# Attention, token mixing and routed experts on one core: separate query buffers for the last rows, earlier queries for the first full pair, a third buffer for a key load

## The chip, the core and the metric

The kernel runs on one NeuronCore of a Trainium2 chip. The metric is the device time of one execution in microseconds (us), here the median of three runs. The engines are named as the profile names them: PE (TensorE; PEld is its weight load), DVE (VectorE), ACT (ScalarE), POOL (GpSimd) and SP (SyncE), which here only issues DMAs. Each engine takes its instructions in the order in which the program gives them to it and waits on semaphores of the others.

## The reference

Attention with a position bias, then two feed-forward blocks. The change lies in the attention; the rest is cut to its signature.

```python
def _attn_ref(q, k, v, w1, b1, w2):          # q, k, v: batch 2, 8 heads, 576 rows, 64 wide
    B, H, S, D = q.shape
    scores = (1.0 / np.sqrt(D)) * np.matmul(q, k.transpose(0, 1, 3, 2))
    pos = np.arange(S)
    psi_rel = np.log1p(np.abs((pos[:, None] - pos[None, :]).astype(np.float32)))
    psi_i = np.log1p(np.maximum(pos[:, None].astype(np.float32), 1.0))
    h = np.maximum((psi_rel / psi_i)[..., None] @ w1 + b1, 0.0)   # 32 hidden values per pair of positions
    scores = scores + (h @ w2).transpose(2, 0, 1)[None]           # one bias per head
    attn = np.exp(scores - np.max(scores, axis=-1, keepdims=True))
    attn = attn / (np.sum(attn, axis=-1, keepdims=True) + 1e-09)
    return np.matmul(attn, v).astype(np.float32)

def reference(**kwargs):
    x = attention output, laid out as batch, row, head * 64
    x = _moe_ref(x, ...)       # mixes tokens, then channels
    return _moe2_ref(x, ...)   # one of 8 experts per token
```

## The kernel before

The attention runs first and is written out as 40 steps, `steps` in `attention`. A step is one block of query rows (`it`) and one `i` from 0 to 7, which names a batch and a pair of heads. The first eight steps (0 to 7) take the block `it = 4`, the last 64 rows of each head: 576 is four blocks of 128 rows and a rest of 64. For them a query tile holds two heads of 64 rows each, both for `hi` and `lo` parts, with zeros in the places of the other head. Steps 8 to 15 take `it = 0`, the first full block of 128 rows, and so on to step 39.

Each step does, for its pair of heads: the score matmuls (`scores`, L359), the bias added and the maximum taken on DVE (L337), the exponential on ACT (L340), the normalisation (L370, L371, and L374 on POOL for the last rows), the transposition of the probabilities (L387, L397, L410), the product with the values (L425) and the transposition of the result (L441). The pieces belong to different steps at a time: step s does the scores of step s, the transpositions of step s - 1 and the values of step s - 2.

Beside that, steps 0 to 7 prepare what comes later:

- **Keys.** `load_k(i)` loads the keys of two pairs by five DMAs (L216 four times, L217) into a ring of two buffers named `kn`; `key_T` transposes them on PE, casts to K on ACT (L193), and `key_split` takes the rests on DVE (L272). There are four loads: 0 and 2 at the start, 4 later in the start, 6 after step 1.
- **Queries.** `load_q` loads them into a ring of two buffers `qn`. For the last rows, one load brings four steps' worth, and `tail_split` (on POOL, L193 and L295) and `tail_T` prepare one step at a time, two steps and one step ahead. For full rows one load brings two steps; `query_T` transposes them on PE (L314) and scales them on ACT into `qr` (L197), `query_split` casts them (L193, on ACT or POOL in turn), and `query_rest` takes the rest on POOL (L325) and issues four DMAs (L328) that lay hi and lo parts out in the query tile `qt0` or `qt1`. The tiles serve the last rows and the full rows alike, so the four DMAs of the first full pair wait for scores of the last rows that read the same tile. `query_zero` (L287, L288) zeroes their empty places once, on POOL.
- **Bias.** The bias of a block of rows is made in eight groups of 16 rows. `bias_hidden` makes the hidden values (L487, L490), `bias_mm` multiplies them (L500), ACT evicts the result into one of two buffers `ev` (L503), and one DMA (L511) lays it out in the block's bias tile. The buffer `ev` of a group may be written again when the DMA of the group two before has landed. One group of block 0 is made in the start, the other seven in steps 0 to 6. Softmax of step 8 needs all eight.

All DMAs named here are issued by SP, in the order in which the code calls them; those on one queue stand behind each other. The order inside a step is a list of names, `ORDER`: "first" for steps 0 to 2, "mixed" for 3 to 7, then "bias" and "edge". The DMA of `load_q` stands ahead of the list, `load_k(6)` and `load_v(1)` behind it. Later stages (token mixing, channel mixing, routing and experts) are not touched by the change.

These are the lines that set when the queries of full rows are prepared and loaded:

```python
QO = 3, 3, 3, 6
two = lambda d: (s + d) % 2 == 0 and s + d >= B * NP and at(d)     # B * NP is 8
"query_T": (query_T, two(QO[0])), "query_split": (query_split, two(QO[1])), "query_rest": (query_rest, two(QO[2])),
if two(QO[3]):
    load_q(*steps[s + QO[3]])
```

So the first full pair (steps 8 and 9) is loaded in step 2 and prepared in step 5; the second pair (10 and 11) is loaded in step 4, into the `qn` buffer that still holds the queries of steps 4 to 7, and prepared in step 7.

Of the kernel before, what the change touches and what calls it, by code (L numbers as in the profile page):

```python
# [9 lines left out]
F32 = mybir.dt.float32  # L10
F32R = mybir.dt.float32r
# [10 lines left out]
B, H, S, D = 2, 8, 576, 64  # L22
# [29 lines left out]
AHEAD = 1  # L52
QRB = 2
TB = 2
QO = 3, 3, 3, 6

ORDER = {
    "start": "hidden0 const load_k2 tail_split0 hidden1 bias0 hidden2 bias1 key_T00 hidden3 zero key_T01 key_T11 key_T10 key_split0 tail_split1 bias2 hidden4 bias3 load_k4 hidden5 key_split1 tail_T bias4 load_v load_q".split(),
    "first": "scores0 hidden2 last_T prob_T0 values key_T0 normalize query_T tail_T query_split hidden1 hidden0 key_T1 bias_mm key_split out_T tail_split hidden3 query_rest".split(),
    "mixed": "hidden2 scores0 values tail_T query_T normalize hidden0 last_T prob_T0 key_T0 key_T1 query_split tail_split hidden1 key_split query_rest bias_mm out_T hidden3".split(),  # L60
    "bias": "query_T query_split hidden3 scores0 scores1 last_T values hidden0 query_rest hidden2 late bias_mm out_T mix prob_T0 prob_T1 hidden1 normalize".split(),
# [71 lines left out]
def attention(tc, nc, tok, mix, q, k, v, w1, b1, w2, c_L, c_id, ident, x, wt1, wt2, prefill):  # L133
# [4 lines left out]
    NP = H // 2  # L138
# [4 lines left out]
    tw_p = pool(tok, "tokw")  # L143
    with ExitStack() as ctx:
        cst = pool(ctx, "acst")
        bias_p = pool(ctx, "bias", 2)
        nat_p = pool(ctx, "nat")
# [5 lines left out]
        def alloc_ps():  # L153
            return ps_t.tile([128, 512], F32, name="tp", tag="tr")
# [40 lines left out]
        def scaled(what, out, in_):  # L195
            if next(turns[what]) == "A":
                nc.scalar.activation(out, in_, AF.Copy, scale=0.125)  # L197
            else:
                nc.vector.tensor_scalar(out, in_, 0.125, None, ALU.mult)  # L199
# [10 lines left out]
        def load_k(i):  # L210

            b, pr = divmod(i, NP)
            n = nat_p.tile([128, 20, D], F32, name="kn", tag="kn", bufs=2)
            main, hs = n[:, 0:16].rearrange("p (n h) d -> p n h d", h=4), k[b, 2 * pr:2 * pr + 4]
            for j in range(NIT):
                nc.sync.dma_start(main[:, j], hs[:, 128 * j:128 * j + 128].rearrange("h p d -> p h d"))  # L216
            nc.sync.dma_start(n[0:64, 16:20], hs[:, 512:S].rearrange("h p d -> p h d"))  # L217
            for j in range(2):
                nat["k", i + j] = main[:, :, 2 * j:2 * j + 2], n[0:64, 16 + 2 * j:18 + 2 * j]
# [14 lines left out]
        def load_q(it, i):  # L234

            b, pr = divmod(i, NP)
            n = nat_p.tile([128, 4, D], F32, name="qn", tag="qn", bufs=2)
            if it == NIT:
                tv = q[b, :, 512:S].rearrange("(a e) p d -> e p a d", e=2)
                for e in range(2):  # L240
                    nc.sync.dma_start(n[64 * e:64 * e + 64], tv[e])
                for j in range(NP):
                    nat["q", it, i + j] = n[:, j]
            else:
                nc.sync.dma_start(n, q[b, 2 * pr:2 * pr + 4, 128 * it:128 * it + 128].rearrange("h p d -> p h d"))
                nat["q", it, i] = n
# [29 lines left out]
        QT = {}  # L276
        qts = [nat_p.tile([128, 2, 4, 128], F32R, name=f"qt{i}") for i in range(2)]

        def query_tile(s):
            return qts[s // 2 % 2][:, s % 2]  # L280

# [1 line left out]

        def query_zero():

            for qt in qts:
                nc.gpsimd.memset(qt[:, :, 0:2, 64:128].bitcast(F32), 0.0)  # L287
                nc.gpsimd.memset(qt[:, :, 2:4, 0:64].bitcast(F32), 0.0)  # L288

        def tail_split(it, i):  # L290
            n = nat.pop(("q", it, i))
# [5 lines left out]

        def tail_T(it, i):
            qs = nat.pop(("qs", it, i)).bitcast(F32).rearrange("p a d -> p (a d)")
            QT[it, i] = qt = query_tile(i)  # L300
            tp = alloc_ps()
            for a in range(2):
                nc.tensor.transpose(tp[:, 128 * a:128 * a + 128], qs[:, D * a:D * a + 128], ident)
            tv = tp[:, 0:256].rearrange("p (a i) -> p a i", a=2)
            scaled("qT0", qt[:, 0:2, 0:64], tv[:, :, 0:64])
            scaled("qT1", qt[:, 2:4, 64:128], tv[:, :, 64:128])
# [277 lines left out]
        steps = [(it, i) for it in its for i in range(B * NP)]  # L584
# [23 lines left out]
        def late_fetch(s):  # L608

            if pieces and any(f is decode for f, *_ in late.get(s, ())):  # L610
                fetch(pieces.pop(0))

        load_const()
        bias_setup()
        start = {
            "const": (bias_const,), "zero": (query_zero,), "load_k2": (load_k, 2), "load_k4": (load_k, 4), "load_v": (load_v, 0),
            "load_q": (load_q, *steps[NP]), "tail_T": (tail_T, *steps[0]),
        }
        for n in range(2):
# [11 lines left out]
        for s in range(N + 2):  # L631

            bias = gi < len(groups) and s < N and s >= B * NP * (its.index(groups[gi] // 8) - 1)
            at = lambda d, n=N: steps[s + d] if 0 <= s + d < n else None
            two = lambda d: (s + d) % 2 == 0 and s + d >= B * NP and at(d)
            hide = groups[gi + 1] if bias and gi + 1 < len(groups) else None
            todo = {
                "late": (late_step, (s,)), "mix": (mixes[s][0], mixes[s][1:]) if s in mixes else (None, None),
                "tail_split": (tail_split, at(2, B * NP)), "tail_T": (tail_T, at(1, B * NP)),
                "query_T": (query_T, two(QO[0])), "query_split": (query_split, two(QO[1])), "query_rest": (query_rest, two(QO[2])),  # L640
                "key_split": (key_split, at(2, B * NP)),
                "normalize": (normalize, at(0)), "last_T": (last_T, at(-1)),
                "values": (values, at(-2)), "out_T": (out_T, at(-2)),
                "bias_mm": (bias_mm, (groups[gi],) if bias else None),
            }
            for j in range(4):
                todo[f"hidden{j}"] = bias_hidden, hide is not None and (hide, (j,))
                todo[f"key_T{j}"] = key_T, j < 2 and at(2, B * NP) and (*at(2), j)
                todo[f"scores{j}"] = scores, at(0) and (*at(0), j)
                todo[f"prob_T{j}"] = prob_T, at(-1) and (*at(-1), j)  # L650
            if two(QO[3]):
                load_q(*steps[s + QO[3]])
            for name in ORDER["edge" if bias and s % (B * NP) == B * NP - 1 else "first" if s < 3 else "mixed" if s < B * NP else "bias" if bias else "plain"]:
                f, a = todo[name]
                if a:
                    f(*(a[1:] if f in (key_split, key_T) else a))
            gi += bias
            late_fetch(s - 1)
            if s == 1:
                load_k(6)  # L660
            if s == 2:
                load_v(1)
            if s == 10:
                prefill()
            if s == 8:
                for _ in range(2):
                    fetch(pieces.pop(0))
# [1095 lines left out]
```

## Time and profile before

| | |
|---|---|
| median of 3 runs | 584.0 us (583.43 to 585.43) |
| the profiled execution, its own time | 584.03 us |
| its span, first to last instruction | 582.3 us |
| mean granted TensorE clock | 0.979 |
| busy: PE, PEld, DVE, ACT, POOL | 545.5 (94%), 430.3 (74%), 383.9 (66%), 329.5 (57%), 242.1 (42%) us |
| chain that ended last, by engine | PE 65%; DVE 12%; DMA 7%; issue 5%; ACT 5% |

The span is what lies between the first and the last instruction of the profiled execution; the rest of its 584.03 us lies around it. PE is busy 94% of the span, but not evenly: in 40 slices of the span, the first five show 7, 6, 8, 9 and 6 tenths and nearly all others 9. The steps 0 to 8 lie there: the scores of step 0 run at 21.6 us, those of step 8 at 64.5 and 66.2 us.

### The profile page before, as it was taken

The page shows a single profiled execution, that of the slowest core. Times are in us where ns is not written, and L with a number is a line of the kernel's source. Part 1 is how long each engine was busy: PE and PEld are TensorE (multiplying, and loading weights), DVE is VectorE, ACT ScalarE, POOL GpSimd, SP SyncE. Part 2 cuts the span into 40 slices and gives each one's busy share as a digit, 9 for nine tenths or more (in the row PEclk, how much of TensorE's full clock was granted, in tenths as well). Part 3 has the DMA queues.
Part 4 walks back from the last instruction along what each step waited for, and adds up shares of the span by engine and source line. Part 5 has one row for each costly group of instructions (what it writes and reads, how often), then busy time and mean ns, then how long its engine had stood idle before and what let it go on. Part 6 is the DMA issues. An engine that isn't in the chain of part 4 may idle for free.

```text
span 582.3 us, 11959 instructions
## 1 busy us (share of the span) xinstructions
PE 545.5 (94%) x4306; PEld 430.3 (74%) x4306; DVE 383.9 (66%) x896; ACT 329.5 (57%) x608; POOL 242.1 (42%) x230
## 2 busy tenths in 40 slices
PE   7689699999899999989999999999999999999992
PEld 3366477777677887869999877787778778787871
DVE  5789588889887675698888535714473235668650
ACT  4678589789898793344444223221423257777760
POOL 4666547476555360044444300310014234657541
PEclk8979889999999999999999999999999999999997
DMA  6997988698697351143443020081002985566950
GB/s 162 130 173 126 142 158 165 132 177 157 127 147 126 77 154 38 37 138 120 148 161 126 1 91 0 1 302 61 19 18 43 370 299 175 147 230 245 367 185 12
DMA packets 72110, 79.90 MB, mean 137 GB/s; under 512 B 36822, under 2 KB 51420, under 8 KB 72044
## 3 DMA queue, kind: packets, MB, share of 16 engines
q1 hardware_dynamic: 67276, 73.72, 50.7%
q0 software_dynamic: 2176, 5.26, 2.7%
q8 instruction: 36, 0.59, 0.5%
q10 hardware_dynamic: 2592, 0.09, 0.3%
q14 instruction: 30, 0.25, 0.2%
HBM read 72.08 MB, written 5.34 MB: 133 GB/s over the span
## 4 chain that ended last, share of the span: by engine, by line
PE 65%; DVE 12%; DMA 7%; issue 5%; ACT 5%; SPq 2%; POOL 2%; ACTq 0%; POOLq 0%; DVEq 0%
PE ph L748 20%; PE po L748 16%; DMA bias<-ev 6%; PE py L748 5%; PE ps L500 5%; PE tp L425 4%; PE ps L359 3%; PE tp L410 3%; DVE t L337 2%; ACT t L340 2%; PE tp L748 1%; DVE K L272 1%; DMA mt<-meta 1%; PE tp L1448 1%; DVE raw L732 1%
## 5 line engine op out<-in xcount | busy, mean ns | idle before, releaser
L490 POOL TENSOR_SCALAR hd<-tabs,sc,negb 128x576 f32<-128x576 f32 x32 | 76.4, 2389 | 4.7 <-PE ps L500 3.0
L340 ACT ACTIVATE t<-t,st 128x576 f32<-128x576 f32 x72 | 55.4, 770 | 28.8 <-DVE st L337 28.4
L748 PE MATMUL po<-cw,h 128*128 128x512 f32 x272 | 67.3, 395 | 0.0
L337 DVE CUSTOM_DVE_ANT_0 t<-ps,bias 128x576 f32<-128x576 f32 x72 | 52.3, 751 | 16.1 <-DMA bias<-ev 6.6
L359 PE MATMUL ps<-K,qt 128*128 128x288 f32 x320 | 54.0, 309 | 4.4 <-DVE qt L199 3.5
L748 PEld LDWEIGHTS po<-cw,h 128*128 128x128 f32 x272 | 49.8, 188 | 10.0 <-issue 0.4
L1411 DVE TENSOR_TENSOR big<-raw,big 128x1024 fp32r<-128x1024 f32 x30 | 42.3, 1433 | 22.4 <-ACT big L1410 22.4
L500 PE MATMUL ps<-hd,wblk 128*32 128x288 f32 x576 | 47.7, 440 | 7.5 <-DVE st L337 6.5
L359 PEld LDWEIGHTS ps<-K,qt 128*128 128x128 f32 x320 | 45.0, 192 | 6.7 <-DVE qt L199 2.3
L425 PE MATMUL tp<-pt,v 128*64 128x128 f32 (+1 forms) x800 | 49.2, 268 | 0.6 <-DVE K L272 0.6
L748 PE MATMUL py<-big,hT 128*128 128x512 f32 x184 | 47.8, 400 | 0.4 <-POOL big L1411 0.4
L1189 POOL DMA_INDIRECT meta<-tokid,posi x10 | 10.0, 996 | 90.7 <-DVE tokid L1186 54.7
L425 PEld LDWEIGHTS tp<-pt,v 128*64 128x64 f32 x800 | 40.1, 137 | 8.1 <-issue 5.1
L1410 ACT CAST big<-raw 128x1024 fp32r<-128x1024 f32 x44 | 44.2, 1055 | 2.8 <-DMA big<-in_moe_w_dram 1.0
L748 PE MATMUL ph<-big,xT 128*128 128x512 f32 x168 | 42.9, 403 | 0.0
L490 DVE TENSOR_SCALAR hd<-tabs,sc,negb 128x576 f32<-128x576 f32 x69 | 42.2, 640 | 1.0 <-PE ps L500 0.9
L748 PEld LDWEIGHTS py<-big,hT 128*128 128x128 f32 x184 | 33.8, 188 | 8.6 <-POOL big L1411 0.9
L740 POOL TENSOR_TENSOR big<-wf,big 128x512 fp32r<-128x512 f32 x12 | 18.8, 1564 | 50.3 <-ACT big L739 50.3
L487 ACT ACTIVATE hd<-tabs,b1c,sc 128x576 f32<-128x576 f32 x43 | 36.9, 866 | 3.8 <-DVE sc L458 3.7
L1411 POOL TENSOR_TENSOR big<-raw,big 128x1024 fp32r<-128x1024 f32 x10 | 27.5, 2747 | 24.9 <-ACT big L1410 24.3
L748 PEld LDWEIGHTS ph<-big,xT 128*128 128x128 f32 x168 | 30.6, 189 | 8.6 <-issue 1.6
L500 PEld LDWEIGHTS ps<-hd,wblk 128*32 128x32 f32 x576 | 17.2, 115 | 24.1 <-DVE st L337 7.9
(302 smaller groups left out, 1204.7 us busy)
## 6 DMA issues: line engine op xcount, KB each, us to landing
raw<-in_moe_w_dram SPq DMA_DIRECT2D x48, 512.0 KB
raw<-in_moe_w_ch_dram SPq DMA_DIRECT2D x24, 512.0 KB
bias<-ev SPq DMA_DIRECT2D x32, 288.0 KB
qt<-qs SPq DMA_DIRECT2D x64, 128.0 KB
lw<-in_moe_w_dram SPq DMA_DIRECT2D x16, 512.0 KB
big<-in_moe_w_dram SPq DMA_DIRECT2D x8, 512.0 KB
lw<-in_moe_w_dram SPq DMA_DIRECT2D x16, 256.0 KB
big<-in_moe_w_dram SPq DMA_DIRECT2D x16, 256.0 KB
```

The costliest lines, as they stand in the source:

```text
L337: nc.vector.tensor_tensor_reduce(t.rearrange("p (a j) -> p a j", a=2), ps[:, :, 0:HALF], bs.rearrange("p (a j) -> p a j", a=2), op0=ALU.ad ...
L340: nc.scalar.activation(t, t, AF.Exp, bias=st[:, j:j + 1], scale=-1.0, accum_out=st[:, 2 + j:3 + j])
L359: nc.tensor.matmul(ps[:, hf, 0:HALF], lhsT=qt[:, j], rhs=K[k][:, hf * HALF:(hf + 1) * HALF], start=j == pairs[0][0], stop=j == pairs[-1][0])
L410: nc.tensor.transpose(tp[:, 128 * j:128 * j + 128], tt[:, o:o + 128], ident)
L425: nc.tensor.matmul(po[64 * h:64 * h + 64, 0:rhs.shape[1]], lhsT=lhsT, rhs=rhs, start=j == 0, stop=j == 4)
L487: nc.scalar.activation(hd[:, qq], Lt[:, o:o + S], AF.Relu, bias=b1c, scale=sc[:, c])
L490: eng.tensor_scalar(hd[:, qq], Lt[:, o:o + S], sc[:, c], negb, ALU.mult, ALU.max)
L500: nc.tensor.matmul(ps[32 * qq:32 * qq + 32, hf, 0:HALF], lhsT=wblk, rhs=hd[:, qq, hf * HALF:(hf + 1) * HALF], start=True, stop=True)
L740: nc.gpsimd.tensor_tensor(lo, src, hi.bitcast(F32), ALU.subtract)
L748: nc.tensor.matmul(out, lhsT=lhs[a], rhs=rhs[b], start=first and i == 0, stop=last and i == 2)
L1410: nc.scalar.copy(hi, raw)
L1411: (nc.gpsimd if c == 3 and t else nc.vector).tensor_tensor(lo, raw, hi.bitcast(F32), ALU.subtract)
```

## The change

Three things:

- The last rows' queries get a tile of their own with two halves, `lastq`, in the place where a later weight tile (`w2s`) is allocated; `tail_T` writes it and `query_zero` zeroes it. `qt0` and `qt1` serve full rows alone.
- The first full pair's queries are prepared in step 4 in place of step 5; the later pairs three steps ahead as before. Their loads stay where they were.
- `load_k(4)` goes into a third buffer (in the place of a later tile `ks`), so that `load_k(6)` uses the buffer of load 0; and `load_k(6)` is called at the end of the start, behind `load_q`, and no longer after step 1.

```diff
-QO = 3, 3, 3, 6
+QO = 3
-    "start": "... load_k4 hidden5 key_split1 tail_T bias4 load_v load_q".split(),
+    "start": "... load_k4 hidden5 key_split1 tail_T bias4 load_v load_q load_k6".split(),
...
         def load_k(i):
             b, pr = divmod(i, NP)
-            n = nat_p.tile([128, 20, D], F32, name="kn", tag="kn", bufs=2)
+            if i == NP:
+                n = nat_p.tile([128, 20, D], F32, name="kn2", tag="ks")
+            else:
+                n = nat_p.tile([128, 20, D], F32, name="kn", tag="kn", bufs=2)
...
         qts = [nat_p.tile([128, 2, 4, 128], F32R, name=f"qt{i}") for i in range(2)]
+        lastq = tw_p.tile([128, 2, 4, 128], F32R, name="lastq", tag="w2s")
...
         def query_zero():
-            for qt in qts:
-                nc.gpsimd.memset(qt[:, :, 0:2, 64:128].bitcast(F32), 0.0)
-                nc.gpsimd.memset(qt[:, :, 2:4, 0:64].bitcast(F32), 0.0)
+            for qt in (lastq[:, 0], lastq[:, 1]):
+                nc.gpsimd.memset(qt[:, 0:2, 64:128].bitcast(F32), 0.0)
+                nc.gpsimd.memset(qt[:, 2:4, 0:64].bitcast(F32), 0.0)
...
-            QT[it, i] = qt = query_tile(i)
+            QT[it, i] = qt = lastq[:, i % 2]
...
-            two = lambda d: (s + d) % 2 == 0 and s + d >= B * NP and at(d)
+            ready = steps[B * NP] if s == B * NP - 4 else s + QO > B * NP and (s + QO) % 2 == 0 and at(QO)
...
-                "query_T": (query_T, two(QO[0])), "query_split": (query_split, two(QO[1])), "query_rest": (query_rest, two(QO[2])),
+                "query_T": (query_T, ready), "query_split": (query_split, ready), "query_rest": (query_rest, ready),
...
-            if two(QO[3]):
-                load_q(*steps[s + QO[3]])
+            if s % 2 == 0 and s + 6 >= B * NP and at(6):
+                load_q(*at(6))
...
-            if s == 1:
-                load_k(6)
```

What SP issues between the end of the start and step 2, before (`v0` are the values of the first batch, `qn` queries, `bias0` the bias tile of block 0, `kn` keys):

```order
L241 DMA qn_336<-in_q_dram 64x4x64 x2
L511 DMA bias0_310<-ev_388 16x8x576
L511 DMA bias0_310<-ev_463 16x8x576
L216 DMA kn_474<-in_k_dram 128x4x64 x4
L217 DMA kn_474<-in_k_dram 64x4x64
L245 DMA qn_480<-in_q_dram 128x4x64
L511 DMA bias0_310<-ev_560 16x8x576
```

and in the changed kernel (its lines have moved by three to five):

```order
L244 DMA qn_337<-in_q_dram 64x4x64 x2
L219 DMA kn_340<-in_k_dram 128x4x64 x4
L220 DMA kn_340<-in_k_dram 64x4x64
L516 DMA bias0_311<-ev_395 16x8x576
L516 DMA bias0_311<-ev_470 16x8x576
L248 DMA qn_481<-in_q_dram 128x4x64
L516 DMA bias0_311<-ev_561 16x8x576
```

The five key DMAs of `load_k(6)` stand ahead of the bias DMAs of steps 0 and 1, behind which they stood.

What SP issues from step 3 to step 6, before: the bias of step 3, the load of the second full pair (`qn_679`, step 4), the bias of step 4, the four query DMAs of the first full pair (step 5), the bias of step 5, a load and the bias of step 6.

```order
L511 DMA bias0_310<-ev_672 16x8x576
L245 DMA qn_679<-in_q_dram 128x4x64
L511 DMA bias0_310<-ev_766 16x8x576
L328 DMA qt0_104<-qs_846 64x2x256 x4
L511 DMA bias0_310<-ev_870 16x8x576
L245 DMA qn_877<-in_q_dram 128x4x64
L511 DMA bias0_310<-ev_944 16x8x576
```

and in the changed kernel:

```order
L516 DMA bias0_311<-ev_673 16x8x576
L248 DMA qn_680<-in_q_dram 128x4x64
L333 DMA qt0_104<-qs_755 64x2x256 x4
L516 DMA bias0_311<-ev_779 16x8x576
L516 DMA bias0_311<-ev_871 16x8x576
L248 DMA qn_878<-in_q_dram 128x4x64
L516 DMA bias0_311<-ev_945 16x8x576
```

The four query DMAs stand behind the same load, and ahead of the bias of step 4, behind which they stood. On ACT, PE and POOL the preparation of that pair (L314, L197, L193, L325) moves from step 5 to step 4; from step 7 on, all engines have the order that they had.

## Rows read from the trace of the kernel before

**Rows 1.** Waits, all engines, 30 to 82 us: total us, times, longest.

```profile
POOL t L374 <- DVE st L371: 10.0, 6, 3.4
...
DVE t L337 <- DMA bias<-ev: 4.9, 1, 4.9
...
PE ps L500 <- DVE st L337: 4.3, 1, 4.3
...
ACT ev L503 <- DMA bias<-ev: 1.2, 1, 1.2
...
PE ps L359 <- DMA qt<-qs: 1.0, 1, 1.0
...
DVE K L272 <- ACT K L193: 0.5, 1, 0.5
```

**Rows 2.** Chain that ended last, around step 8: start us, us, what.

```profile
57.65 5.64 DMA bias<-ev
...
63.37 0.75 ACT ev L503
...
64.14 7.37 DMA bias<-ev
...
71.73 0.76 DVE t L337
```

**Rows 3.** Timeline of SP: start us, us, engine, line, operation, count.

```profile
11.48 8.94 SPq L509 DMA_DIRECT2D bias<-ev  x8
20.52 2.25 SPq L216 DMA_DIRECT2D kn<-in_k_dram  x4
...
34.48 1.28 SPq L511 DMA_DIRECT2D bias<-ev  x2
35.85 3.96 SPq L216 DMA_DIRECT2D kn<-in_k_dram  x4
39.85 1.47 SPq L217 DMA_DIRECT2D kn<-in_k_dram  x1
...
57.65 1.66 SPq L511 DMA_DIRECT2D bias<-ev  x1
59.48 2.66 SPq L328 DMA_DIRECT2D qt<-qs  x4
```

**Rows 4.** Timeline of POOL, two instructions (in brackets the idle time before).

```profile
16.58 3.18 POOL L490 TENSOR_SCALAR hd<-tabs,sc,negb 128x576 f32<-128x576 f32 x1 [1.41 <-PE ps L500]
...
56.82 0.32 POOL L295 TENSOR_TENSOR qm<-qn,qm 128x64 fp32r<-128x64 f32 x1
```

**Rows 5.** Waits of the DMA queue of SP, 33 to 76 us.

```profile
SPq L245 <- POOL qm L295: 3.7, 1, 3.7
```

**Rows 6.** Timeline of ACT, steps 2, 3 and 5.

```profile
40.09 0.73 ACT L503 ACTIVATE ev<-ps,cb 128x576 f32<-128x576 f32 x1
40.71 0.86 ACT L487 ACTIVATE hd<-tabs,b1c,sc 128x576 f32<-128x576 f32 x1
42.97 0.78 ACT L340 ACTIVATE t<-t,st 128x576 f32<-128x576 f32 x1 [1.40 <-DVE st L337]
...
55.15 0.38 ACT L197 ACTIVATE qr<-tp 128x256 f32<-128x256 f32 x1
...
57.20 0.62 ACT L193 CAST qs<-qr 128x512 fp32r<-128x512 f32 x1
```

**Rows 7.** Chain that ended last, a bias DMA of the next block of rows.

```profile
106.16 4.07 DMA bias<-ev
```

**Rows 8.** Stretches: us, busy PE, PEld, DVE, ACT, POOL (count), granted clock, DMA share, GB/s.

```profile
57.50:59.50 2.00, 2.00 (x31) 1.72 (x29) 1.86 (x6) 1.98 (x4) 1.61 (x2) 1.00 0.30 64
59.50:64.20 4.70, 4.70 (x69) 3.42 (x67) 4.35 (x15) 3.38 (x7) 2.68 (x6) 1.00 0.99 167
64.20:71.60 7.40, 3.05 (x38) 2.34 (x35) 1.10 (x4) 2.78 (x6) 4.31 (x4) 0.84 1.14 142
72.50:76.00 3.50, 3.45 (x23) 1.63 (x24) 3.26 (x10) 2.45 (x6) 0.00 (x0) 0.50 0.34 80
```

More of the change, by code (lines that the diff above doesn't have):

```diff
@@ L54 @@
 TB = 2
-QO = 3, 3, 3, 6
+QO = 3
 ORDER = {
-    "start": "hidden0 const load_k2 tail_split0 hidden1 bias0 hidden2 bias1 key_T00 hidden3 zero key_T01 key_T11 key_T10 key_split0 tail_split1 bias2 hidden4 bias3 load_k4 hidden5 key_split1 tail_T bias4 load_v load_q".split(),
+    "start": "hidden0 const load_k2 tail_split0 hidden1 bias0 hidden2 bias1 key_T00 hidden3 zero key_T01 key_T11 key_T10 key_split0 tail_split1 bias2 hidden4 bias3 load_k4 hidden5 key_split1 tail_T bias4 load_v load_q load_k6".split(),
     "first": "scores0 hidden2 last_T prob_T0 values key_T0 normalize query_T tail_T query_split hidden1 hidden0 key_T1 bias_mm key_split out_T tail_split hidden3 query_rest".split(),
@@ L615, in attention @@
         start = {
-            "const": (bias_const,), "zero": (query_zero,), "load_k2": (load_k, 2), "load_k4": (load_k, 4), "load_v": (load_v, 0),
+            "const": (bias_const,), "zero": (query_zero,), "load_k2": (load_k, 2), "load_k4": (load_k, 4), "load_k6": (load_k, 6), "load_v": (load_v, 0),
             "load_q": (load_q, *steps[NP]), "tail_T": (tail_T, *steps[0]),
```

## Prediction

> **What bounds the kernel now.** I read the waits first, then the chain, then the queue of SP. The change touches steps 0 to 8 alone, so the question is what ends last there. The waits show one large stall: the softmax of step 8 on DVE waits 4.9 us for a bias DMA, and PE, whose next bias group needs the PSUM that this softmax empties, stands 4.3 us behind it; PE's wait for the first full pair's queries is only 1.0 us [rows 1]. The chain says why the bias is late. Call the bias DMA issued in step s B(s). B(4) is issued at 57.65 and lands 5.64 later; only then may ACT evict the next group into the same `ev` buffer (63.37, 0.75 us); B(6) goes out at 64.14 and lands at 71.51; the softmax starts at 71.73 [rows 2]. And B(4) is issued so late because SP stood 3.7 us at the load ahead of it, the second full pair's [rows 5], until POOL had split the queries of step 7, whose buffer that load overwrites: POOL ends at 57.14 [rows 4], the load goes out right behind, and B(4) at 57.65 [rows 3]. After step 8 PE is the bound, and the order is as before on every engine; a shift of that softmax is carried to the end, so the sum is made on it.
>
> **The change part by part**, against the profiled execution's own 584.03 us (the median of the runs is 584.0; 0.3% of it is 1.75 us, about what a measurement here can tell from no change).
>
> *Own buffers for the last rows.* They take waits on scores off the four query DMAs. Those DMAs went at 59.48, as soon as B(4), ahead of them on SP, was out (57.65 and 1.66) [rows 3]; no wait on scores shows. Value 0. The four zeroings are half as large on POOL; POOL stands 1.41 us shortly after, waiting for PE [rows 4], so 0. If that cover were gone, it would be a gain of under 1.41.
>
> *Third key buffer.* `load_k(4)` no longer waits for transpositions. Before, it started at 20.52, right behind the eight bias DMAs that end at 20.42 [rows 3]: no wait there. Value 0. It only lets `load_k(6)` come earlier.
>
> *`load_k(6)` earlier.* Five DMAs now stand ahead of B(0) and B(1). Who waits for B(0)? The eviction of step 2, on the same `ev` buffer, which ran at 40.09; 0.62 later the next hidden part starts (0.86), and behind both stands the exponential of step 3, at 42.97, 1.40 us after ACT was free [rows 6]. So the eviction may start up to 41.5 without harm. B(0) went at 34.48. Five key DMAs take 2.8 (the four at 20.52 take 2.25) to 5.47 (35.85 to 41.32) [rows 3], so B(0) goes at 37.3 to 39.95. The long case had two bias DMAs ahead of it, which now stand behind, so I take 37.3. A bias DMA needs 4.07 [rows 7] to 5.64 [rows 2] from issue to landing; middle 4.86, so 42.2. The eviction then starts some 0.7 us after 41.5, the exponential 0.8 late, and with it DVE, POOL and what they feed. Bounds: 37.3 and 4.07 give 0; 39.95 and 5.64 give 45.6, 4.1 late. Value **+0.8** (0 to +4.1).
>
> *Queries one step earlier.* On ACT two operations (0.38 and 0.62 [rows 6]) go from step 5 to step 4. In step 4 only the 0.38 stands ahead of the key casts that DVE takes up at once: up to 0.4 late. In step 5 DVE had waited 0.5 for those casts [rows 1], which goes. Value 0 (-0.5 to +0.4). POOL has one subtraction more in step 4 and one fewer in step 5; it waits for DVE in each of these steps, 10.0 us in six of them [rows 1], so 0. PE's two transpositions move alike and lie within the same bounds.
>
> *The queue at step 4.* The load of the second full pair still waits for POOL's split of step 7: its buffer is the same. So it goes as before, behind POOL's 57.14 (plus what came earlier), and now the four query DMAs (2.66 [rows 3]) stand between it and B(4), which is issued at about 60.4 and not at 57.65. With 4.07 to 5.64 it lands at 64.5 to 66.0, not 63.29; eviction and issue take 0.85, B(6) goes at 65.3 to 66.9, and with the same 4.07 to 5.64 lands at 69.4 to 72.5. But a floor holds: from 59.5 on the DMA engines are busy all the time (shares 0.99 and 1.14) until B(6) lands [rows 8], and the bytes up to B(6) are the same in either order; only the stretch 57.5 to 59.5, at share 0.30 [rows 8], could be filled better, and its load stands first in both. So hardly below 71.4. Between 71.4 and 72.5 I stay near the floor, because B(6) is queued behind work that is still running and needs no time alone: 71.6, **+0.1** (-2.1 to +1.0; the low end if the shares were no bound). The 1.0 us that PE waited for queries goes, and is worth 0: PE would stand as long for the softmax.
>
> Sum: 0.8 + 0 + 0.1 = +0.9, 584.03 + 0.9 = **584.9**.
>
> One rule of the Trainium skill speaks for more. The page "DMA: Bandwidth & Descriptors", section "Anatomy of one DMA — SWDGE (gpsimd) path", fits a DMA as about 2.0 us fixed plus its bytes over 436 GB/s, which for the 288 KB of a bias DMA would be an estimated 2.7 us; with that, B(6) would land near 67. The section fits another issuing path than SP's, and the trace here has 5.64 for one with almost nothing ahead of it, so the sum above uses the rows.
>
> **The rivals.**
>
> - *A, faster.* The DMA engines are no floor: they show as busy with waiting small pieces, and the order decides. Then B(4) lands 4.07 after 60.4, at 64.5, B(6) goes at 65.3 and lands at 69.4 in place of 71.51, and no key load delays step 2: -2.1, 581.9; a little less if step 2 slips. For it: B(4) hid no other transfer before, and now its flight lies under the queries'. Against it: the shares of 1 [rows 8]. This is the case that the skill's fit would make larger.
> - *B, slower.* The five key DMAs take as long as they did at 35.85, so B(0) goes at 39.95, lands at 44.8, and the exponential of step 3 is 3.4 late. It decides from about a landing at 43.2 on, where 1.75 us are lost. Time 584.03 + 3.4 + 0.1 = 587.5. For it: that slow issue is in the trace. Against it: the other key load took 2.25 for four.
> - *C, slower.* The clock. After PE's stand the granted clock is 0.50 from 72.5 to 76.0 [rows 8]: 3.5 us of work at half speed, which costs 1.75. PE now stands longer, because the scores of step 8 no longer wait for queries and the softmax is later. If the clock stays down that long once more, 1.75 come on top: 584.9 + 1.75 = 586.7.
> - *D, nothing.* B(0) lands in time and the queue's floor holds: 584.0. The change then takes away waits that were not last.
>
> **How the numbers follow.** Forecast 0.50, D 0.13 (both within 0.3%: 0.63); A 0.10 (faster); B 0.13 and C 0.14 (slower: 0.27). The likeliest is the forecast, 584.9. The range leaves out A's case and the larger part of B: 583.0 to 587.0.
>
> **What would show it right or wrong.** In the changed profile: the waits should have no PE wait for `qt<-qs` in step 8, but still a DVE wait of 4 us or more for `bias<-ev`, since B(6) lands no earlier. The chain should again run through two bias DMAs and an eviction between, the first issued near 61. SP's wait at L248 for POOL should still be there. An eviction of step 2 near 42, with a wait for a bias DMA that was not there before, shows the +0.8; without it D, near 45 B. The granted clock at 72 to 80 tells C. I am wrong if the DVE wait for the bias shrinks to under 3 us, or if the steps 3 to 7 run with another period.

## The result, and the profile after

The change makes the kernel slower: 587.55 us (583.98 to 588.46, 22 runs) against 583.27 us (582.03 to 585.53, 22 runs) for the kernel before, ratio of the runs 1.0057, 95% interval 1.0045 to 1.0069, so about 3.3 us by the ratio (the two medians lie 4.3 apart). The forecast was +0.9, 584.9 us, with a range of 583.0 to 587.0: the median lies above the range, and so does 584.03 times the ratio, 587.4. The profiled execution of the changed kernel took 586.64 us with a span of 584.8 (before 584.03 and 582.3).

The whole difference lies ahead of step 8: its first softmax pass on DVE starts at 74.38 us for 71.73 [rows 2], 2.65 late, and the span is 2.5 longer. (Lines of the changed kernel are 3 to 5 numbers higher: L342 is the softmax pass, L345 the exponential, L508 the eviction to `ev`, L516 a bias DMA, L505 the bias matmuls, L364 scores, L248 the load of a full pair's queries, L333 the query DMAs, L219 and L220 key loads. In the runs further below they move by a few numbers again.)

Waits of the changed kernel, 30 to 82 us, all engines (total us, times, longest), beside [rows 1]:

```profile
DVE st L375 <- ACT t L345: 6.5, 3, 4.4
ACT ev L508 <- DMA bias<-ev: 4.0, 1, 4.0
ACT ev L508 <- PE tp L392: 3.1, 1, 3.1
...
PE ps L364 <- ACT ev L508: 2.4, 1, 2.4
DVE t L342 <- POOL qs L330: 2.1, 1, 2.1
...
PE ps L505 <- DVE st L342: 0.8, 1, 0.8
```

New is a wait of 3.1 us ahead of an eviction on ACT: that of step 2. It is put down to a PE transposition (42.69 to 43.33) that this eviction does not read; what it reads, the bias matmuls of step 2, had ended at 39.62. The other thing that it needs is the `ev` buffer that B(0) reads, and it starts as B(0) lands; in other runs below the same wait is put down to the bias DMA. PE's wait for `qt<-qs` is gone, as forecast. DVE's 4.9 us for the bias are no longer listed, though DVE still stands as long: between steps 7 and 8 it stood 4.39 behind an exponential that ACT could do only after the late eviction of step 6 (4.0 us for B(4)), then 2.11, together 6.50; before, 1.55 and 4.87, together 6.42. The 2.11 are put down to POOL, but the pass starts 0.2 us after B(6) lands. Timelines of DVE, the kernel before and then the changed one:

```profile
65.66 0.15 DVE L370 TENSOR_SCALAR st<-st 128x1 f32<-128x1 f32 x1 [1.55 <-ACT t L340]
...
71.73 0.76 DVE L337 CUSTOM_DVE_ANT_0 t<-ps,bias 128x576 f32<-128x576 f32 x1 [4.87 <-DMA bias<-ev]
```

```profile
71.07 0.15 DVE L375 TENSOR_SCALAR st<-st 128x1 f32<-128x1 f32 x1 [4.39 <-ACT t L345]
...
74.38 0.76 DVE L342 CUSTOM_DVE_ANT_0 t<-ps,bias 128x576 f32<-128x576 f32 x1 [2.11 <-POOL qs L330]
```

Timeline of SP in the changed kernel (start us, us, engine, line, operation, count), beside [rows 3]:

```profile
34.52 2.20 SPq L219 DMA_DIRECT2D kn<-in_k_dram  x4
36.76 1.62 SPq L220 DMA_DIRECT2D kn<-in_k_dram  x1
38.48 1.29 SPq L516 DMA_DIRECT2D bias<-ev  x2
...
60.24 0.38 SPq L248 DMA_DIRECT2D qn<-in_q_dram  x1
60.72 3.10 SPq L333 DMA_DIRECT2D qt<-qs  x4
63.93 1.25 SPq L516 DMA_DIRECT2D bias<-ev  x2
```

Timeline of ACT in step 2 and at the exponential of step 3, beside [rows 6]:

```profile
43.38 0.74 ACT L508 ACTIVATE ev<-ps,cb 128x576 f32<-128x576 f32 x1 [3.08 <-PE tp L392]
44.02 0.86 ACT L492 ACTIVATE hd<-tabs,b1c,sc 128x576 f32<-128x576 f32 x1
44.78 0.76 ACT L345 ACTIVATE t<-t,st 128x576 f32<-128x576 f32 x1
```

B(0) goes out 4.0 us later (38.48 for 34.48), the eviction starts 3.29 later (43.38 for 40.09), the exponential 1.81 later (44.78 for 42.97). Up to the load of the second full pair the lateness is 3.07 (60.24 for 57.17), so another 1.26 came in between. 0.4 of it goes with the queries' preparation, which now stands in step 4: at full clock and with that preparation, the kernel with the keys back (below) takes 14.60 us from that exponential to the load, the kernel before 14.20. The rest comes with a fall of PE's clock. Stretches of the changed kernel (columns as in [rows 8]):

```profile
46.00:49.00 3.00, 2.13 (x30) 1.82 (x29) 2.86 (x9) 2.94 (x5) 2.72 (x4) 1.00 1.22 142
49.00:53.00 4.00, 3.20 (x31) 2.10 (x31) 3.69 (x14) 2.88 (x7) 2.37 (x5) 0.93 1.15 198
53.00:57.00 4.00, 4.00 (x42) 2.85 (x35) 2.69 (x6) 3.16 (x5) 3.32 (x4) 0.65 0.64 119
```

Before, the granted clock was 1.00 in all of this. Here PE stood several times behind the late step, and then ran at 0.50 (the 1.2 GHz level) for some 3 us: sixteen bias matmuls took 2.01 us for 1.18, eight score matmuls 2.00 for 1.31.

From the load on, the chain that ended last runs as [rows 2] did:

```profile
63.93 4.77 DMA bias<-ev
...
68.78 0.75 ACT ev L508
...
69.55 2.72 DMA bias<-ev
72.27 1.98 issue
...
74.38 0.76 DVE t L342
```

From the load to step 8's pass it is 14.14 us now and was 14.56: after the load the new order of the queue is worth 0.4 us less time, not more, about what the preparation in step 4 cost ahead of it.

### The profile page after: what moved, and what is told of

The parts are those of the page before. It is cut to its first block, busy times and chain, and to the rows that moved or that the text cites. A ratio compares the mean times of both kernels' runs of the same rounds, so it can differ in the third digit from the quotient of the medians.

```text
span 584.8 us, 11953 instructions
## 1 busy us (share of the span) xinstructions
PE 550.0 (94%) x4306; PEld 434.3 (74%) x4306; DVE 389.9 (67%) x896; ACT 329.5 (56%) x608; POOL 246.1 (42%) x230
## 4 chain that ended last, share of the span: by engine, by line
PE 69%; DVE 10%; issue 5%; ACT 5%; DMA 5%; SPq 2%; POOL 1%; ACTq 0%; POOLq 0%; DVEq 0%
PE ph L751 21%; PE po L751 16%; PE py L751 6%; PE ps L505 5%; DMA bias<-ev 5%; PE tp L430 5%; PE ps L364 4%; PE tp L415 3%; ACT t L345 2%; DVE t L342 2%; PE tp L751 1%; PE tp L1451 1%; PE tp L446 1%; DVE raw L735 1%; PE tp L1547 1%
## 5 line engine op out<-in xcount | busy, mean ns | idle before, releaser
L345 ACT ACTIVATE t<-t,st 128x576 f32<-128x576 f32 x72 | 55.4, 770 | 25.7 <-DVE st L342 25.5
L342 DVE CUSTOM_DVE_ANT_0 t<-ps,bias 128x576 f32<-128x576 f32 x72 | 52.2, 750 | 14.8 <-PE ps L364 5.3
L1414 DVE TENSOR_TENSOR big<-raw,big 128x1024 fp32r<-128x1024 f32 x30 | 47.2, 1596 | 16.1 <-ACT big L1413 14.7
L505 PE MATMUL ps<-hd,wblk 128*32 128x288 f32 x576 | 49.2, 447 | 4.0 <-DVE st L342 3.1
L364 PE MATMUL ps<-K,qt 128*128 128x288 f32 x256 | 44.4, 315 | 2.4 <-ACT ev L508 2.4
L364 PEld LDWEIGHTS ps<-K,qt 128*128 128x128 f32 x256 | 36.9, 196 | 2.7 <-ACT ev L508 2.6
L508 ACT ACTIVATE ev<-ps,cb 128x576 f32<-128x576 f32 x36 | 26.6, 738 | 18.9 <-PE ps L505 8.3
L1414 POOL TENSOR_TENSOR big<-raw,big 128x1024 fp32r<-128x1024 f32 x10 | 25.9, 2588 | 20.1 <-ACT big L1413 20.0
```

Of the source, the lines that this page charges most:

```text
L342: nc.vector.tensor_tensor_reduce(t.rearrange("p (a j) -> p a j", a=2), ps[:, :, 0:HALF], bs.rearrange("p (a j) -> p a j", a=2), op0=ALU.ad ...
L345: nc.scalar.activation(t, t, AF.Exp, bias=st[:, j:j + 1], scale=-1.0, accum_out=st[:, 2 + j:3 + j])
L364: nc.tensor.matmul(ps[:, hf, 0:HALF], lhsT=qt[:, j], rhs=K[k][:, hf * HALF:(hf + 1) * HALF], start=j == pairs[0][0], stop=j == pairs[-1][0])
L505: nc.tensor.matmul(ps[32 * qq:32 * qq + 32, hf, 0:HALF], lhsT=wblk, rhs=hd[:, qq, hf * HALF:(hf + 1) * HALF], start=True, stop=True)
L508: nc.scalar.activation(ev.rearrange("p (a b) -> p a b", a=2), ps[:, :, 0:HALF], AF.Identity, bias=cbs[hidden_by(g).replace("P", "V")])
L1414: (nc.gpsimd if c == 3 and t else nc.vector).tensor_tensor(lo, raw, hi.bitcast(F32), ALU.subtract)
```

## The experiments

Two theories went in. **K:** the key loads ahead of B(0) delay the eviction of step 2 through the two `ev` buffers. **Q:** the four query DMAs ahead of B(4) cost the time. The traces' main points, in us (for the exponential, the eviction and the pass their starts); executions differ by up to 1.3 us from the start on, so the first column gives the bias matmuls of step 1 for comparison:

| kernel | matmuls of step 1 | B(0) issued | eviction, step 2 | exponential, step 3 | load, second pair | first pass, step 8 | ratio to before (95%) |
|---|---|---|---|---|---|---|---|
| before | 32.14 | 34.48 | 40.09 | 42.97 | 57.17 | 71.73 | 1 |
| changed | 32.16 | 38.48 | 43.38 | 44.78 | 60.24 | 74.38 | 1.0057 (1.0045 to 1.0069) |
| changed, again | 32.03 | 37.30 | 44.91 | 46.31 | 60.90 | 75.04 | one run |
| keys back | 32.25 | 35.21 | 40.45 | 43.27 | 57.87 | 72.61 | 1.0001 (0.9977 to 1.0025) |
| keys only | 32.26 | 37.60 | 44.98 | 46.38 | 60.55 | 74.88 | 1.0030 (1.0000 to 1.0059) |
| third `ev` | 30.85 | 36.12 | 39.15 | 42.03 | 56.64 | 70.93 | 0.9989 (0.9964 to 1.0014) |
| two keys | 32.08 | 35.63 | 42.54 | 43.94 | 58.58 | 73.38 | 1.0034 (1.0006 to 1.0061) |
| third `qn` | 31.73 | 34.05 | 39.62 | 42.50 | 52.31 | 68.48 | 0.9967 (0.9941 to 0.9993) |

**Keys back.** The changed kernel with `load_k6` taken out of `ORDER["start"]` again and the load behind step 1.

```diff
+            if s == 1:
+                load_k(6)
```

> The changed kernel with one part undone: load_k(6) goes back behind step 1 (its third key buffer, the last rows' buffers and the preparation in step 4 stay). Theory K (the five key DMAs ahead of B(0) delay the eviction of step 2, and the clock falls behind it): the eviction of step 2 is back near 40.1 us (43.4 in the changed kernel), no half clock between 49 and 57, the load of the second full pair goes near 57.2 (60.2), and the time is 0.4 us under that of before: 582.9 us, ratio 0.998 to 1.001. Theory Q (the four query DMAs ahead of B(4) cost the time): step 8's first DVE pass stays near 74.4, ratio 1.0045 to 1.007.

583.23 us, ratio 1.0001: the loss is gone, with the step-4 preparation and both sets of buffers still there. The eviction of step 2 is at 40.45 without a wait. Timeline of ACT:

```profile
40.45 0.73 ACT L508 ACTIVATE ev<-ps,cb 128x576 f32<-128x576 f32 x1
...
43.27 0.78 ACT L345 ACTIVATE t<-t,st 128x576 f32<-128x576 f32 x1 [1.33 <-DVE st L342]
```

Q falls. From the load to step 8's pass it is 14.74 us, 0.2 more than before, where the changed kernel had 0.4 less: the queue's order is worth nothing that can be told apart.

**Keys only.** The kernel before with this part alone: `load_k6` at the end of `ORDER["start"]`, and

```diff
-            n = nat_p.tile([128, 20, D], F32, name="kn", tag="kn", bufs=2)
+            if i == NP:
+                n = nat_p.tile([128, 20, D], F32, name="kn2", tag="ks")
+            else:
+                n = nat_p.tile([128, 20, D], F32, name="kn", tag="kn", bufs=2)
...
-            if s == 1:
-                load_k(6)
```

> The kernel before with this part of the change alone: load_k(6) at the end of the start, into a third key buffer. Theory K: the eviction of step 2 near 43.4 us, half clock around 49 to 57, the load of the second full pair near 60.2 and the whole loss of 3.1 to 3.7 us, ratio 1.005 to 1.0065. Theory Q: as before, ratio 0.999 to 1.001.

585.79 us, ratio 1.0030: slower, by less than expected, with an interval that reaches from 0 to the whole loss. The one execution traced has all of it (load 3.4 late, step 8's pass 3.15). Timeline of ACT, and two stretches of the same kernel:

```profile
44.98 0.74 ACT L506 ACTIVATE ev<-ps,cb 128x576 f32<-128x576 f32 x1 [5.06 <-DMA bias<-ev]
...
46.38 0.76 ACT L343 ACTIVATE t<-t,st 128x576 f32<-128x576 f32 x1
```

```profile
44.00:46.00 2.00, 0.23 (x3) 0.15 (x6) 0.00 (x0) 1.02 (x2) 0.00 (x0) 1.00 0.59 51
46.00:48.00 2.00, 1.61 (x16) 0.38 (x10) 0.70 (x3) 2.00 (x5) 0.21 (x1) 1.00 0.54 90
```

Here the wait is put down to the bias DMA, as it should be. PE was busy 0.23 of 2 us and the clock stayed at 1.00 through it, up to 74.9 us; the fall to half is not a fixed part of the loss.

**Third `ev` buffer.** The changed kernel, each DMA in its place.

```diff
-            ev = nat_p.tile([128, S], F32, name="ev", bufs=2)
+            ev = nat_p.tile([128, S], F32, name="ev", bufs=3)
```

> The changed kernel with a third ev buffer; every DMA keeps its place in SP's order. Theory K, by way of the ring of two ev buffers: the eviction of step 2 no longer waits and ends near 41, the clock stays at full between 49 and 57, the load of the second full pair goes near 57.2, and the eviction of step 6 doesn't wait for B(4) either, so that B(6) is issued near 64: step 8's first DVE pass at 70 to 72 us against 74.4, ratio 0.996 to 1.001 to the kernel before. If the early key DMAs cost time in another way (DMA engines shared with other loads), the eviction moves and the ratio stays above 1.003. Theory Q: ratio 1.0035 to 1.007, since SP's order at step 4 is the same.

582.68 us, ratio 0.9989. With the key loads still ahead of B(0), neither the eviction of step 2 nor that of step 6 waits, and the loss is gone. So it passed through the two `ev` buffers. The same run shows a floor: B(6) goes out at 62.39, 5.9 us earlier than in the changed kernel once the starts are put level (1.31), and lands about 70.7, only 2.1 earlier by the same count, with the queries, B(4), B(5) and a load issued ahead of it.

**Two of five key DMAs ahead of B(0).**

```diff
-... "load_k6": (load_k, 6), ...
+... "load_k6": (load_k, 6, (0, 1)), ...
...
+            if s == 1:
+                load_k(6, (2, 3, 4))
```

> The changed kernel with two of the five key DMAs of load_k(6) at the end of the start and three behind step 1. Theory K with a linear price: B(0) is issued near 35.7 us and lands near 40.3, since two DMAs take 1.2 us on SP; the eviction of step 2 then comes near 40.5 for 43.4, inside the 1 us of slack that ACT has there, the clock stays at full, and nothing of the loss is left: ratio 0.999 to 1.002. If any load ahead of B(0) costs its own time, 2 of 5 keep two fifths of the loss, 1.2 us, ratio 1.002 to 1.003; theory Q, the whole loss, 1.005.

585.75 us, ratio 1.0034 (1.0006 to 1.0061); I had expected nothing, or two fifths of the loss if each load has its own price. By the ratio it is more than that, though the interval holds two fifths too; step 8's pass is 1.65 late in the trace. SP did what I said, the landing didn't. Timelines of SP and of ACT:

```profile
34.43 1.10 SPq L222 DMA_DIRECT2D kn<-in_k_dram  x2
35.63 1.29 SPq L520 DMA_DIRECT2D bias<-ev  x2
```

```profile
42.54 0.74 ACT L512 ACTIVATE ev<-ps,cb 128x576 f32<-128x576 f32 x1 [1.93 <-DMA bias<-ev]
...
43.94 0.76 ACT L349 ACTIVATE t<-t,st 128x576 f32<-128x576 f32 x1
```

B(0) went at 35.63, 1.15 us later than before, and landed 6.9 us after it, for 4.7 in the kernel before. What the loads cost is thus not SP's issue time alone; B(0) is also longer under way behind them.

**The changed kernel again**, for a second profile.

> The changed kernel once more, for a second profile of it. Theory K says that its time goes with the landing of B(0): with the eviction of step 2 near 43.4 again about 586.5 us, near 45 about 587 to 588. If the fall of the clock between 52.6 and 56 is part of the change's cost, it is there again; if it was one draw, the eviction near 45 comes with a load of the second full pair near 60.5 at full clock.

586.93 us in its one run. Timelines of SP, ACT and PE:

```profile
34.36 2.20 SPq L219 DMA_DIRECT2D kn<-in_k_dram  x4
36.60 0.61 SPq L220 DMA_DIRECT2D kn<-in_k_dram  x1
37.30 1.55 SPq L516 DMA_DIRECT2D bias<-ev  x2
```

```profile
44.91 0.74 ACT L508 ACTIVATE ev<-ps,cb 128x576 f32<-128x576 f32 x1 [4.50 <-DMA bias<-ev]
...
46.31 0.76 ACT L345 ACTIVATE t<-t,st 128x576 f32<-128x576 f32 x1
```

```profile
45.70 2.88 PE L505 MATMUL ps<-hd,wblk 128*32 128x288 f32 x16 [1.07 <-ACT ev L508]
```

SP issues B(0) at 37.30, to the digit what I had forecast; it lands 7.6 us later, at about 44.9, where I had 42.2. The clock fell here too, but at another place (0.50 between 46 and 49). From the exponential of step 3 to the load it is 14.59 us here, as with the keys back, so this fall cost nothing there.

The traces also hold 16 completion marks for each DMA, and a DMA has landed with the last of them. For B(0), the fifteenth and the sixteenth, in us from its issue (the eviction that waits starts 0.1 us behind the sixteenth):

| kernel | loads ahead | fifteenth mark | sixteenth mark |
|---|---|---|---|
| before | 0 | 4.7 | 4.7 |
| changed | 5 | 4.8 | 4.8 |
| changed, again | 5 | 5.4 | 7.5 |
| keys only | 5 | 5.5 | 7.3 |
| third `ev` | 5 | 5.4 | 7.2 |
| two keys | 2 | 5.0 | 6.8 |

Up to the fifteenth mark B(0) needs 0.1 to 0.8 us more than before. In the last four kernels the greater part, 1.8 to 2.1 us, is one mark alone; on the last key load ahead of B(0) one mark already came 3.0 to 3.6 behind the other fifteen there, and 0.5 in the first profile. The marks don't say whether it is the same DMA engine each time, and why it lags stays open.

**Spare matmuls on PE.** The changed kernel with 16 and 15 transposes of `ident`, written over afterwards, where PE stood; then with 5 and 5.

```diff
+            for _ in range(16 * ((it, i) == steps[1])):
+                nc.tensor.transpose(tp[:, 0:128], ident, ident)
             nc.tensor.transpose(tp[:, 0:128], o, ident)
```

> The changed kernel, DMA order and all, with 31 spare transposes of ident on PE (results written over): 16 ahead of the transpose of out_T in step 3 and 15 ahead of the second half of step 4's prob_T, where PE stood 0.87 and 0.80 us. If the half clock between 52.6 and 56 comes of these stands, it stays at full, the bias matmuls of step 4 take 1.18 us for 2.01 and the score matmuls 1.31 for 2.00, and the load of the second full pair goes 1 to 1.4 us earlier after the same eviction of step 2 (43.4): time 585 to 586.5 us. If the clock falls for another reason, both matmul groups stay near 2.0 us and the load moves by less than 0.3.

> The changed kernel with 5 and 5 spare transposes for 16 and 15: at 0.12 us each (1.86 us for 15) they fill 0.6 us of each stand and don't reach past it. If the clock falls for these stands and the eviction of step 2 comes near 43.4, the bias matmuls of step 4 take 1.2 us and not 2.0 and the load of the second full pair goes 1 us earlier (59.2), time 585 to 587 us. If B(0) lands near 45, as in two of the runs above, PE stands longer elsewhere and the run says nothing on this.

The first is a miss: 591.76 us in its one run. Its timeline of PE:

```profile
49.00 2.85 PE L449 MATMUL tp<-ident 128*128 128x128 f32 x16 [0.32 <-DVE pt L193]
...
54.71 1.86 PE L390 MATMUL tp<-ident 128*128 128x128 f32 x15
```

I had taken a transpose at half of its time; it is 0.12 us at full clock, so both groups ran past the stands, and the clock was already down at the first; the eviction of step 2 came at 45.43 besides. The smaller dose took 584.6 us in its one run, with the eviction at 42.92 and full clock up to step 8 (bias matmuls of step 4 in 1.18 us). But its load came 2.41 late for an eviction 2.83 late. From the exponential of step 3 to the load it took 15.26 us at full clock, against 15.46 in the changed kernel and 14.60 with the keys back: what the clock gave back is nearly hidden by the time of the spare matmuls themselves. How much of the loss is the clock's stays open; it is at most those 0.9 us, and none in the second profile.

**Third `qn` buffer**, on the kernel with the keys back: the wait of SP at L248 for POOL (6.8 us in the changed kernel, 4.0 with the keys back, 3.7 before [rows 5]) is taken away.

```diff
-            n = nat_p.tile([128, 4, D], F32, name="qn", tag="qn", bufs=2)
+            n = nat_p.tile([128, 4, D], F32, name="qn", tag="qn", bufs=3)
```

> The kernel of the first of these runs (load_k(6) back behind step 1) with a third qn buffer, so that the load of the second full pair has no wait for POOL's split of step 7 and B(4) no longer stands behind it on SP. If that wait sets B(4), and B(4)'s landing the eviction of step 6 and so B(6): the load goes near 53 instead of 57.2, B(4) near 56, the eviction of step 6 near 62.2 without a wait, B(6) lands near 67.2, and step 8's first DVE pass is at 67 to 69 us against 71.7 before: 3 to 5 us gained, and up to 1.8 more if PE's clock does not fall between 68 and 76: 577 to 581 us, ratio 0.989 to 0.996. If the DMA engines are the floor of step 8 (as my prediction took it for the queue at step 4), B(6) still lands past 70.5 and the ratio is 0.998 to 1.001.

580.97 us, ratio 0.9967: faster than both kernels; the time is at the end of what I expected, the ratio (0.9941 to 0.9993) a little short of it. Timeline of SP:

```profile
52.31 0.52 SPq L248 DMA_DIRECT2D qn<-in_q_dram  x1
53.35 2.60 SPq L333 DMA_DIRECT2D qt<-qs  x4
56.06 2.77 SPq L516 DMA_DIRECT2D bias<-ev  x2
58.92 0.54 SPq L248 DMA_DIRECT2D qn<-in_q_dram  x1
63.83 0.55 SPq L516 DMA_DIRECT2D bias<-ev  x1
```

Load, queries and B(4) go 5 to 6 us earlier than with the keys back alone, and step 8's pass comes 2.8 us earlier than before with the starts put level. The clock still fell to 0.50 between 70 and 74.

**Both buffers**, with `load_k(6)` in the two `kn` buffers as before and every third of the first evictions in the buffer of tag `ks`.

```diff
+            if groups.index(g) % 3 == 2 and groups.index(g) < 14:
+                ev = nat_p.tile([128, S], F32, name="ev2", tag="ks")
+            else:
+                ev = nat_p.tile([128, S], F32, name="ev", bufs=2)
```

> The kernel with the third qn buffer and load_k(6) behind step 1 in the two kn buffers, as before the change; of the first 14 groups' evictions every third goes to the buffer of tag ks, which is free until wt1_s, so ev has three buffers there. If the eviction of step 6 is held by B(4)'s landing alone (1.43 us with two ev buffers), it now starts near 61.6 us for 63.06, B(6) is issued near 62.4 and lands near 66.8, and step 8's first DVE pass comes near 67.0 for 68.5 (start taken equal); PE then stands 1.5 us less, and if the clock doesn't fall at 68 to 75 another 1 to 1.5 us go: 1.5 to 3 us under the kernel with qn alone, 578 to 579.5 us, ratio 0.990 to 0.9945 to the kernel before. If DMA engines still busy with the queries set B(6), it lands past 68 and the ratio is 0.995 to 0.998.

579.72 us, ratio 0.9925 (0.9893 to 0.9956). The eviction of step 6 waits for nothing and B(6) goes out 2.0 us earlier than with the third `qn` alone, starts put level; but it lands 5.67 us after its issue, and step 8's pass comes 0.75 earlier. More than half of what the earlier issue gave went into the longer flight (4.44 us with the third `qn` alone).

**The later load.** The same with the load that stood between B(5) and B(6) behind B(6).

```diff
-            if s % 2 == 0 and s + 6 >= B * NP and at(6):
+            if s % 2 == 0 and s + 6 >= B * NP and at(6) and s != 6:
...
+            if s == 6:
+                load_q(*at(6))
```

> The kernel with the third qn buffer and the third ev buffer, with the load of the pair of step 12 (issued between B(5) and B(6), 128 KB) moved behind B(6). If what holds B(6) there is the DMA engines at work on what stands ahead of it, B(6) lands 0.7 to 1.2 us earlier after the bias matmuls of step 6 (66.75 against 58.36 in that kernel's trace) and step 8's first DVE pass comes 0.7 to 1 us earlier: ratio 0.990 to 0.995. If B(6) is at its own floor of some 4.3 us from issue to landing already, this changes at most 0.3 us.

> The kernel of the later load once more, since its ratio came from four runs alone: by step 8's first pass in its trace (66.0 against 71.7 us before, with a start 1 us earlier in that execution) 4.5 to 6 us under the kernel before, ratio 0.988 to 0.993; at 0.995 or above the first ratio was a good draw.

577.2 us, ratio 0.9877 (0.9843 to 0.9911) from four runs, and 577.91 us, 0.9911 (0.9892 to 0.9930), when repeated: the fastest of all, over 5 us under the kernel before. The later load's own part is not told apart from nothing: the intervals overlap that of the kernel with both buffers. Chain at step 8, first execution and repeat:

```profile
61.25 4.59 DMA bias<-ev
...
66.01 0.76 DVE t L339
```

```profile
60.64 5.08 DMA bias<-ev
...
65.88 0.76 DVE t L339
```

With one load of 128 KB moved behind it, B(6) landed 4.59 and 5.08 us after its issue, for 5.67. With the starts put level, step 8's pass came 1.18 us earlier than with both buffers in the first execution and 0.15 in the repeat.

**Queries in step 3**, on top of that.

```diff
-            ready = steps[B * NP] if s == B * NP - 4 else s + QO > B * NP and (s + QO) % 2 == 0 and at(QO)
+            ready = steps[B * NP] if s == B * NP - 5 else s + QO > B * NP and (s + QO) % 2 == 0 and at(QO)
```

> The kernel with both buffers and the later load, with the first full pair's queries prepared in step 3 instead of step 4, so that their four DMAs go ahead of B(3) and not of B(4). If the DMA engines are the floor of step 8 from about 55 us on, these 3.6 us of queries leave the stretch: B(4), B(5) and B(6) land 4.3 to 5 us after their issue, and step 8's first pass comes 0.5 to 1.5 us earlier than with the later load alone; ratio 0.987 to 0.993. If the queries ahead of B(3) hold up the eviction of step 5 in the way in which the key loads held up that of step 2 (three ev buffers make that unlikely), nothing is gained or some is lost.

584.24 us, ratio 0.9994 (0.9972 to 1.0016): all of the gain is lost, and not for the reason that I had in mind. Waits of PE, 36 to 56 us:

```profile
PE tp L316 <- DMA qn<-in_q_dram: 4.5, 1, 4.5
```

The first pair's load goes out in step 2 behind the key loads and had not landed. PE takes its work in order here: all of step 3 stood behind two transpositions (L316, started at 47.10), and the clock was 0.50 from 46 to 49 us and 0.59 from 49 to 53. I had moved the user and forgotten the load.

## Why the prediction was right or wrong

- **Own buffers, third key buffer: 0.** Not contradicted: with the keys back both are there and the ratio is 1.0001, which holds them together with the two terms at step 4 below.
- **Queries one step earlier: 0 (-0.5 to +0.4).** The two shifts that I named are there: the exponential of step 5 comes 0.4 late in the keys-back kernel, that of step 6 is level again (17.18 us after that of step 3, for 17.28 before). But the load of the second pair waits for a split that POOL does in step 5, ahead of the time that comes back. So it pays the 0.4: from the exponential of step 3 to the load it is 14.60 us with the keys back, 14.61 with the third `ev`, 14.64 with two keys and 14.59 in the second profile, for 14.20 before and 14.17 with the keys only, the two kernels that leave the preparation in step 5.
- **`load_k(6)` earlier: +0.8. This is the step that failed.** Its mechanism held at each link: five DMAs ahead of B(0), the eviction of step 2 waiting for B(0), some 1.4 us of slack behind it. The eviction is 3.29 and 4.82 late in the two profiles of the change, 4.89 in the keys-only run and 2.45 in the two-keys run, and the exponential of step 3 is 1.81, 3.34, 3.41 and 0.97 late: 1.48 is hidden each time.

  Mis-sized was the landing of B(0), 42.2 in the sum: it came at about 43.4 and 44.9. In the first profile SP was late, with an issue at 38.48 for 37.3, and the flight was the 4.9 of the sum; in the second the issue was the 37.3 of the sum, and the flight took 7.6, 2.1 of it one lagging completion mark.

  So the 4.07 to 5.64 us that the sum gives a bias DMA from issue to landing was too narrow behind key loads: 4.9 to 7.6 there. Those two rows were of bias DMAs with little ahead of them, and [rows 2] itself shows one of 7.37, B(6), which had more ahead.

  I asked whether the DMA engines were a floor at step 4, where it mattered to the queue, and not at step 0, where the loads stood ahead. The trace of before had a sign of it: the engines' share is 1.07 from 36 to 40 us (the stretch below), with B(0) and B(1) under way.

  At the exponential the term came to 1.81 and 3.34 us for 0.8, inside its bounds (0 to +4.1); at the load of the second pair the kernel is 3.07 and 3.73 late, with the 0.4 of the preparation in both and up to 0.9 of half clock in the first.

  Stretch of the kernel before (columns as in [rows 8]):

```profile
36.00:40.00 4.00, 3.93 (x58) 2.80 (x58) 3.69 (x12) 3.09 (x7) 2.17 (x4) 1.00 1.07 146
```

- **Rival B** had the right price, in the second profile by another cause. It let B(0) go out at 39.95 and land at 44.8; B(0) went at 37.30 and landed at 44.9 there, the exponential 3.34 late where B says 3.4. In the first profile SP did issue late, at 38.48, and the exponential was 1.81 late. That its 587.5 us is nearly the measured median is luck: B counts from 584.03, and the kernel before had a median of 583.27 beside the changed one. I gave it 0.13 because only SP's issue spoke for it.
- **Queue at step 4: +0.1.** Right in size: 14.14 us from the load to step 8's pass in both profiles of the change, 14.74 with the keys back, 14.56 before. The third `ev` buffer bears out the floor that spoke against rival A: B(6) issued 5.9 earlier landed only 2.1 earlier.
- **Rival C.** The clock did stay down longer: the stretch from 76 to 80 us has 0.54 in the changed kernel (below), and 0.99 before. But step 9's first pass is 3.12 late (80.11 for 76.99) after a step 8 that was 2.65 late, and step 10's 2.86, so it cost 0.2 to 0.5 us here and not 1.75. That is not general: in the two-keys run, at 0.50 from 76 to 80 us too, step 10's pass is 2.78 late (84.16 for 81.38) after a step 8 that was 1.65 late. The fall between 52 and 56 us, which I had not foreseen, cost at most 0.9 in the first profile and is not there in the keys-only run.

  Stretch of the changed kernel:

```profile
76.00:80.00 4.00, 4.00 (x26) 2.58 (x19) 2.42 (x8) 2.81 (x7) 0.00 (x0) 0.54 0.72 159
```

- **My sign that I am wrong if the DVE wait for the bias shrinks to under 3 us** was badly chosen. The wait went from the list and the time stayed, part of it an engine earlier.

The page "DMA: Bandwidth & Descriptors" of the Trainium skill, section "Queues, rings and completion order", has the rule that I should have weighed: what SP issues runs in one ring on each DMA engine, and descriptors are consumed there in ring order. The runs agree in part: B(0) took 4.7 us from issue to landing with no new loads ahead, 6.9 behind two and 4.9 to 7.6 behind five, but up to the fifteenth mark only 4.8 to 5.5 behind any of them; most of the rest is the mark that lags.

## What to carry to other kernels

A load moved earlier on a queue is paid for by what is now behind it: price its landing from rows of transfers that had as much ahead of them, not only its issue, look at the last of its completion marks, and do so wherever the queue is crossed. Then look for the buffer that ties the late transfer to an engine: one more buffer there (`ev`) took the whole loss away, and one more where the queue's head waited for another engine (`qn`) took 2.3 us off the median of the kernel with the keys back. When a user moves earlier, its load has to move first.

## What was not expected of the hardware

- A like stall brings PE's clock down in one execution and not in another: 0.50 between 46 and 49 us in the second profile, with PE busy 0.93 of 2 us from 44 to 46, and 1.00 in the keys-only run, with PE busy 0.23 of the same 2 us. In the first profile the clock fell later, between 52 and 56.
- The same kernel issued and landed B(0) differently from one execution to the next: 38.48 and 4.9 us, then 37.30 and 7.6 us. The fifth key DMA kept SP for 1.62 us in the first and for 0.61 in the second.
- One of a DMA's 16 completion marks can come 3 us behind the others, and then one comes late on the next DMA as well: 3.0 to 3.6 us on the last key load ahead of B(0) in four runs, 1.8 to 2.1 on B(0).
